# A decay tile in place of a third transpose, and one C Bᵀ burst a block, in a Mamba-2 scan with SwiGLU

## The chip, the cores and the metric

The kernel runs on one core of one Trainium2 chip. The metric is the device time of an execution in microseconds, lower being better. The core has five engines that run their own instruction lists side by side: TensorE (PE, the matrix engine; the profile shows its weight loads apart as PEld), VectorE (DVE), ScalarE (ACT), GpSimd (POOL) and SyncE (SP), which here issues nearly all transfers.[...]

## The reference

There are two parts. The first is a scan with a decaying state (Mamba-2), for 4 batches, 8 heads, 768 steps, 32 values a head (x) and 16 states (B and C). The second is a SwiGLU layer over the 3072 tokens of 256 values that come out of it.

```python
for c in range(nc):                      # chunks of 32 steps
    cum = np.cumsum(la, axis=-1)         # la = log(a), per head
    L = np.exp(cum[..., :, None] - cum[..., None, :]) * causal
    M = np.einsum('bhin,bhjn->bhij', Cc, Bc) * L
    y_intra = np.einsum('bhij,bhjd->bhid', M, xc)
    y_inter = np.einsum('bhin,bhnd->bhid', Cc, state) * np.exp(cum)[..., None]
    y[:, :, sl] = y_intra + y_inter
    Bx = np.einsum('bhjn,bhjd->bhjnd', Bc, xc) * np.exp(cum[..., -1:] - cum)[..., None, None]
    state = np.exp(la.sum(-1))[..., None, None] * state + Bx.sum(2)
# then, on the 3072 x 256 tokens
xn = x / np.sqrt(np.mean(x * x, -1, keepdims=True) + 1e-6) * rms_g
g, val = xn @ w_gate, xn @ w_val         # 256 -> 1536
out = (g / (1 + np.exp(-g)) * val) @ w_out
```

The inputs' weights come as 64-bit numbers in the kernel's view and are turned into fp32 on the chip.

## The kernel before, in words

**Tiling.** Tokens are worked in six blocks of 512 (NBLK). A block is two *pairs*; a pair is two chunks of 128 tokens of one batch, all eight heads side by side (8 heads x 16 states fill the 128 partitions). From pair 2 on, a chunk of 128 is worked as two halves of 64 tokens, so that the masked matrices are 64 x 64. There are 12 pairs, numbered 0 to 11; block b holds pairs 2b and 2b+1.

**A pair's steps**, with the names that the order uses:

- `bc`, `x`: the pair's B, C and x are loaded.
- `scale` (line 484): VectorE makes Bd, B times the decay from each token to the end of its chunk, and Cd, C times the decay from the chunk's start to each token.
- `turn` (line 499): TensorE transposes B, C and (from pair 2 on) Cd of one chunk through the identity into one PSUM bank `tp`, so three transposes a chunk. `T` copies the transposed B and Cd into tile T on ScalarE (line 505), `Tt` the transposed C twice, each time with the heads of one parity set to zero (line 1034, through `turned_of`).
- `g` (line 536): TensorE forms C Bᵀ of all heads of the pair: 16 small products on tiles of 32 x 64 of the array, each issued in two records. The results lie in a pair of banks and two single ones.
- The decay matrices L are made two blocks ahead: `row`/`rowout` store the rows of running sums to DRAM, `spread` loads them back over the partitions, `sub` and `ex` subtract and take the exponential, and GpSimd's select sets what lies ahead of a token to zero.
- `L`, `L1` (lines 556, 562): VectorE multiplies C Bᵀ by L, two heads' pairs at once from the pair of banks and the rest one bank at a time.
- `A` (line 582): TensorE sums Bᵀ x over a chunk's tokens; `S` (lines 596 to 606) carries the state on.
- `y` (line 656): TensorE adds the state's part (from Cdᵀ) and the chunk's own part. The `additions` for pair p+1 are issued at the end of pair p's y, into free columns of the same banks.
- `sq`, `yt`: ScalarE takes squares and copies y out of PSUM; `ms`, `rs`, `xn` norm the tokens of a block.

**The SwiGLU layer.** From block 1 on (and for half of block 0) each group of four products over two row blocks, two columns and two halves of the tokens is formed by seven products of sums (`P.1` to `P.7`, line 844, with `take`, line 850, `C`, line 856, `silu`, line 865, and `hid`, line 869); the output layer does the same (`O.1` to `O.7`, line 934, with sums `s`, `s2`, `s3`, `s4`). The sums of weights are made once (`cw`, line 814, `two`, line 890), those of tokens per block (`tx`). Block 0 also uses plain products (`early`, line 770, `gate`, line 760, `o`, line 876), while `pow`, `man` and `wt` turn the loaded weights into fp32.

**The order.** Nothing is planned at run time: one list, written out by hand, names every step as `block:step`, and each engine gets its instructions in the order of that list. A step `1:turn.0.1` belongs to the next block's pair while block 1's products run, so the scan of block b+1 is laced into the products of block b. SP's transfers stand in the list as well (`fetch` for weights, `bc`, `x`, `spread`, `out`), and one that has to wait for its buffer holds up those behind it. PSUM has two pairs of banks in the first stage (slots 0 and 1, later two for gate and two for val), one further pair (slot 2) and two single banks that all scan steps share.

Of the kernel before, what the change touches and what calls it, by code (L numbers as in the profile page):

```python
# [20 lines left out]
def kernel(  # L21
# [33 lines left out]
    nc = tc.nc  # L55
# [357 lines left out]
    def pair_tile(g):  # L413
        p = g // 2
        if p not in Ls:
            Ls[p] = ssd.tile([P, 2, NH, P if p < 2 else HC], FP32, tag="L", name="L", bufs=2)
        return Ls[p][:, g % 2]
# [60 lines left out]
    def scale(p):  # L478
        s = st[p]
        b, c0 = divmod(2 * p, NC)  # L480
        hs = slice(b * NH, (b + 1) * NH)
        for name, src, d in (("Cd", "C", to_i), ("Bd", "B", from_j)):
            s[name] = ssd.tile([P, 2, NH, N], FP32, tag=name, name=name)
            nc.vector.tensor_tensor(
                out=s[name], in0=s[src],
                in1=d[:, c0:c0 + 2, hs].unsqueeze(3).to_broadcast([P, 2, NH, N]), op=ALU.mult)
# [7 lines left out]
    def turn(p, i, parts=3):  # L494

        s = st[p]
        ps["t", p, i] = tp = bank("tp", (P, parts, P))
        for k, src in enumerate((s["B"], s["C"], s.get("Cd"))[0:parts]):
            nc.tensor.transpose(out=tp[:, k], in_=src[:, i].rearrange("p h n -> p (h n)"),  # L499
                                identity=ident)  # L500

    def turned(p, i, copy):
        tp = ps["t", p, i]
        if tp.shape[1] == 3:
            copy(out=transposed(p)[:, i, 0::3], in_=tp[:, 0::2])
        else:
            copy(out=transposed(p)[:, i, 0], in_=tp[:, 0])

    def turned_of(p, i, t, scaled):

        scaled(transposed(p)[:, i, 1 + t], ps["t", p, i][:, 1], tmask[:, t:t + 1])
# [11 lines left out]
    def product(p, todo):  # L523
        T = st[p]["T"]
        for i in range(2):
            for q, g in todo:
# [8 lines left out]
                for u in halves:  # L535
                    nc.tensor.matmul(  # L536
                        out=g[u, P * i:P * i + P].rearrange("p (t m) -> p t m", t=2),
                        lhsT=T[r, i, 0, u], rhs=T[r, i, 1:3, u], start=(i == 0), stop=True,
# [7 lines left out]
    def products_at_once(p, g):  # L546

        ps["g", p, 0] = g
        ps["g", p, 2], ps["g", p, 3] = g2, g3 = bank("g2", (P, 512)), bank("g3", (P, 512))
        product(p, [(0, g[:, 0]), (1, g[:, 1]), (2, g2), (3, g3)])  # L550

# [92 lines left out]
    def outputs(p, y):  # L644

        if p < 2:
            return first_outputs(p, y)
        s = st[p]
        ps["y pair", p] = y
        y = [y[:, 0], y[:, 1], bank("y2", (P, 512)), bank("y3", (P, 512))]  # L650
        ps["y", p] = y
        first = (2 * p) % NC == 0
        opened = set()

        def product_y(k, u, i, rows, **operands):
            nc.tensor.matmul(out=y[2 * k + u][rows, i * HC:(i + 1) * HC],  # L656
# [4 lines left out]
        for i in range(2):  # L661
            for u in range(2):
                for q in range(NQ):
                    if first and i == 0 and u == 0:
# [13 lines left out]
        if 2 <= p < NPAIR - 1:  # L678
            additions(p + 1, [y[u][:, P:2 * P].rearrange("p (i t d) -> p i t d", i=2, t=2)
                              for u in range(2)])  # L680
        del st[p], Ls[p]

    def parts_of_y(p):
        y = ps["y", p]
        return [(0, slice(0, 2), ps["y pair", p][:, :, 0:P])] + [
            (1, slice(u, u + 1), y[2 + u][:, 0:P].unsqueeze(1)) for u in range(2)]

    def squares(p):
# [3 lines left out]
        tk = slice(half * 256, half * 256 + 256)  # L692
# [5 lines left out]
        sq2 = nrm.tile([P, 2, 2, 2, HC], FP32, tag="sq2", name="sq2", bufs=1)  # L698
        for k, us, y in parts_of_y(p):
            nc.scalar.activation(out=sq2[:, k, :, us].rearrange("p i u m -> p u i m"),  # L700
                                 in_=y.rearrange("p u (i m) -> p u i m", i=2), func=AF.Square)
        s2 = sq2.rearrange("p k i u m -> p k (i u m)")
        nc.gpsimd.tensor_tensor(out=sqs[blk][:, tk], in0=s2[:, 0], in1=s2[:, 1], op=ALU.add)

    def taken_out(p, copy):
# [3 lines left out]
        tk = slice(half * 256, half * 256 + 256)  # L709
# [5 lines left out]
        for k, us, y in parts_of_y(p):  # L715
            copy(out=yts[blk][:, k, tk].rearrange("p (i u m) -> p u i m", i=2, u=2)[:, us],
                 in_=y.rearrange("p u (i m) -> p u i m", i=2))
# [287 lines left out]
    def row_sums(k):  # L1005

        ps["row", k] = r_ps = bank("r_ps", (P, P))
        nc.tensor.matmul(out=r_ps, lhsT=laf[:, 2 * k * BH:(2 * k + 4) * BH], rhs=mid,
                         start=True, stop=True)

    def row_store(k):
        c = 2 * k
        r_sb = nrm.tile([P, P], FP32, tag="r_sb", name="r_sb", bufs=2)
        nc.vector.tensor_copy(out=r_sb, in_=ps.pop(("row", k)))
        nc.sync.dma_start(out=rowd[:, c * BH:(c + 4) * BH].rearrange("u r m -> r u m"),
                          in_=r_sb.rearrange("r (u m) -> r u m", u=2))

# [14 lines left out]
    rowv = rowd.rearrange("u r m -> u (r m)")  # L1032
    def by_scalar(out, in_, scale):
        ac.activation(out=out, in_=in_, func=AF.Copy, scale=scale)

    def by_vector(out, in_, scale):
# [10 lines left out]
        "scale": scale, "turn": lambda p, i: turn(p, i, 3 if p > 1 else 2),  # L1047
        "T": lambda p, i: turned(p, i, ac.copy if p else dv.tensor_copy),
        "Tt": lambda p, i, t: turned_of(p, i, t, by_scalar if p else by_vector),
# [5 lines left out]
        "y": lambda p: outputs(p, take("y", ("y", p))),  # L1055
# [16 lines left out]
        "row": row_sums, "rowout": row_store,  # L1072
# [15 lines left out]
    def of_chunk(n, fn):  # L1088
# [9 lines left out]
        "turn": of_pair(1, turn), "T": of_pair(1, lambda p, i: turned(p, i, ac.copy)),  # L1098
        "Tt": of_pair(1, lambda p, i, t: turned_of(p, i, t, by_scalar)),
        "scale": of_pair(1, scale),  # L1100
        "g": of_pair(1, lambda p: products_at_once(p, pair_of_banks("g", 2))),
        "L": of_pair(1, lambda p: decayed(p, 0)),
        "L1": of_pair(1, decayed_one),
        "A": of_pair(1, additions), "S": of_pair(1, states),
        "y": of_pair(1, lambda p: outputs(p, pair_of_banks("y", 2))),
        "sq": of_pair(1, squares), "yt": of_pair(1, lambda p: taken_out(p, ac.copy)),
# [11 lines left out]
        0:aT 0:la0 0:log4.0.4 0:fetch.7 0:log 0:mask.1.1/2 0:log4.4.2 0:log4.6.2 0:sel 0:upto2  # L1118
        0:after2 0:whole 0:r.0 0:tmask 0:parts.0 0:middles 0:c*2 0:turn.0.1 0:T.0.1 0:cx 0:kinks
        0:eps 0:Tt.0.1.0 0:d 0:dx 0:fetch.8 0:Tt.0.1.1 0:sums.0.1 0:exp.0.1 0:turn.0.0 0:Tt.0.0.0  # L1120
        0:T.0.0 0:Tt.0.0.1 0:scale.1 0:cc 0:sums.0.0 0:exp.0.0 0:mean 0:turn.1.0 0:never16 0:g.0.1/0
        0:L.0.1 0:turn.1.1 0:bc.3 0:T.1.1 0:Tt.1.0.1 0:Tt.1.1.1 0:Tt.1.0.0 0:T.1.0 0:Tt.1.1.0
        0:fetch.9 0:sums.1.1 0:exp.1.1 0:g.0.0/1 0:scale.0 0:last.0 0:Tl.0 0:L.0.0 0:pow.0 0:man.0
        0:A.0 0:S.0 0:bc.4 0:row.1 0:rowout.1 0:man.1 0:wt.0 0:g.1.1/0 0:A.1 0:S.1 0:last.1 0:pow.1
        0:L.1.1 0:Tl.1 0:pow.2 0:mask.1.0/2 0:sums.1.0 0:exp.1.0 0:row.0 0:g.1.0/1 0:mask.3/0
        0:pow.5 0:man.5 0:fetch.10 0:r.1 0:y.0/2 0:sq.0 0:pow.3 0:L.1.0 0:y.1/1 0:sq.1 0:wt.1
        0:scale.2 0:rowout.0 0:man.2 0:pow.6 0:yt.0 0:ydone.0 0:turn.2.0 0:early.0.0/2 0:parts.1
        0:sums.3 0:exp.3 0:ms.0 0:rs.0 0:wt.2 0:pow.4 0:yt.1 0:ydone.1 0:early.0.1 0:mask.2/0
        0:sums.2 0:turn.2.1 0:man.3 0:wt.5 0:wt.3 0:early.1.0/1 0:early.1.1 0:man.4 0:fetch.11
        0:man.6 0:fetch.14 0:scale.3 0:exp.2 0:pow.7 0:xn.0 0:wt.6 0:T.2.0 0:T.2.1 0:Tt.2.1.0  # L1130
        0:Tt.2.1.1 0:Tt.2.0.0 0:Tt.2.0.1 0:table.0 0:x.3 0:wt.4 0:gate.2/0 0:man.8 0:man.7
        0:fetch.13 0:norm.0 0:norm.1 0:wt.7 0:gg.2/2 0:L1.2.3 0:L1.2.2 0:silu.0 0:hid.0 0:L.2.0
        0:tx.0 0:gate.3/1 0:pow.9 0:silu.2 0:hid.2 0:man.9 0:fetch.15 0:A.2 0:S.2 0:pow.8 0:wt.8
        0:silu.3 0:hid.3 0:wt.9 0:pow.10 0:man.11 0:cw.3 0:gate.4/2 0:silu.4 0:hid.4 0:man.10
        0:pow.11 0:wt.11 0:turn.3.1 0:turn.3.0 0:T.3.0 0:Tt.3.0.1 0:T.3.1 0:Tt.3.0.0 0:Tt.3.1.1
        0:Tt.3.1.0 0:wt.10 0:switch.0 0:P.1.3 0:take.1.3 0:x.4 0:gate.5/1 0:silu.5 0:hid.5
        0:fetch.12 0:pow.12 0:y.2/2 0:spread.10 0:spread.11 0:S.3 0:sq.2 0:yt.2 0:ydone.2 0:P.6.3
        0:take.6.3 0:man.13 0:man.12 0:switch.1 0:P.2.3 0:P.1.4 0:pow.13 0:gg.3/2 0:L.3.0 0:L1.3.2
        0:L1.3.3 0:P.2.4 0:silu.1 0:scale.4 0:C.11.3 0:silug.11.3 0:take.1.4 0:fetch.19 0:P.7.3
        0:wt.12 0:take.7.3 0:y.3/2 1:S.0 0:sq.3 0:yt.3 0:ydone.3 0:spread.8 0:P.5.3 0:C.22.3  # L1140
        0:silug.22.3 0:pow.14 0:P.4.3 0:silug.21.3 0:tok 0:tokout 0:P.3.3 0:cw.4 0:P.6.4 0:ms.1
        0:fetch.18 0:wt.13 0:take.6.4 0:C.12.3 0:P.2.5 0:silug.12.3 0:pow.15 0:C.11.4 0:silug.11.4
        0:P.5.4 0:P.7.4 0:take.7.4 0:fetch.16 0:man.14 0:wt.14 0:o.0/2 0:pow.16 0:hid.1 0:o.1
        0:P.4.4 0:silug.21.4 0:cw.5 0:hidg.22.3 0:hidg.11.3 0:hidg.12.3 0:C.22.4 0:hidg.21.3 0:P.1.5
# [173 lines left out]
```

## Time and profile before

| | |
|---|---|
| median of 3 runs | 409.12 us (409.10 to 409.29) |
| the profiled execution | 409.49 us, of which the span 407.4 |
| TensorE busy | 399.9 us (98%) |
| VectorE busy | 303.7 us (75%) |
| ScalarE busy | 231.9 us (57%) |
| GpSimd busy | 37.5 us (9%) |
| moved by DMA | 23.91 MB |

Times in the views are microseconds from the span's start. A row of a list of instructions gives start, duration (first start to last end), engine, line, operation, tile written from tiles read, and the count of records. A row of the groups gives count, then busy time, mean duration in ns, then the engine's idle time just before them and what ended it. Ends on TensorE are modelled and matmuls overlap, so that its rate is read from starts. A 32-bit matmul stands as two records.

### The profile page before, as it was taken

What the parts mean: (1) busy time and instruction counts of PE and PEld (TensorE: products, weight loads), DVE (VectorE), ACT (ScalarE), POOL (GpSimd) and SP (SyncE); (2) the same over time, 40 slices, a digit from 0 to 9 for tenths busy, and PEclk for the clock granted to TensorE, in tenths of its full rate; (3) what the DMA queues carried; (4) which work ended last, traced back from release to release, by engine and by line L of the source; (5) the groups of instructions that cost most, each with busy time, mean ns of one, the idle gap of its engine ahead of it and who ended that gap; (6) DMA issues with size and microseconds to landing.
All of it is one profiled execution on the core that took longest, in us unless ns stands there. A gap on an engine that the chain in (4) does not pass through costs nothing.

```text
span 407.4 us, 9550 instructions
## 1 busy us (share of the span) xinstructions
PE 399.9 (98%) x3867; PEld 340.4 (84%) x3867; DVE 303.7 (75%) x698; ACT 231.9 (57%) x506; POOL 37.5 (9%) x61
## 2 busy tenths in 40 slices
PE   8999999999899999999999999999999999999997
PEld 4566577888688899888899988899988899988997
DVE  5999999898976787856799278779455777265863
ACT  3899989795556445664584355534566442453500
POOL 4010000003200001300023000001300000000000
PEclk9999999999999999999999999999999999999999
DMA  9998937400401171302080501020300000100001
GB/s 112 231 213 173 266 118 209 53 0 5 75 0 28 29 126 39 44 1 55 20 131 8 79 2 53 2 80 2 77 2 0 2 4 0 53 1 2 0 2 52
DMA packets 87371, 23.91 MB, mean 59 GB/s; under 512 B 76800, under 2 KB 81152, under 8 KB 87328
## 3 DMA queue, kind: packets, MB, share of 16 engines
q1 hardware_dynamic: 83168, 23.05, 26.9%
q10 hardware_dynamic: 4160, 0.26, 0.8%
q8 instruction: 30, 0.49, 0.5%
q14 instruction: 13, 0.11, 0.1%
HBM read 20.02 MB, written 3.28 MB: 57 GB/s over the span
## 4 chain that ended last, share of the span: by engine, by line
PE 90%; DVE 4%; ACT 3%; DMA 1%; issue 1%; SPq 0%; ACTq 0%
PE gate L844 27%; PE o L934 22%; PE val L844 20%; PE o L876 4%; PE gate L760 3%; PE y L656 3%; PE tp L499 2%; PE gate L770 2%; PE g L536 1%; PE ms L725 1%; DVE sw L814 1%; DVE s L907 1%; DMA L<-rowd 1%; PE e L422 1%; ACT e L183 1%
## 5 line engine op out<-in xcount | busy, mean ns | idle before, releaser
L856 DVE TENSOR_TENSOR c<-val,p 128x512 f32<-128x512 f32 x99 | 67.6, 688 | 46.3 <-PE val L844 27.5
L850 ACT COPY p<-gate 128x512 f32<-128x512 f32 x99 | 57.4, 586 | 52.4 <-PE gate L844 49.2
L844 PE MATMUL gate<-tx,sw 128*128 128x256 f32 x264 | 65.5, 381 | 0.0
L865 ACT ACTIVATE c<-c 128x256 f32<-128x256 f32 x99 | 39.9, 417 | 41.8 <-DVE c L856 41.6
L844 PEld LDWEIGHTS gate<-tx,sw 128*128 128x128 f32 x264 | 49.1, 190 | 7.0 <-ACT p L850 0.3
L869 DVE TENSOR_TENSOR h<-c 128x256 f32<-128x256 f32 x99 | 41.4, 433 | 17.4 <-ACT c L865 17.3
L844 PE MATMUL val<-tx,sw 128*128 128x256 f32 x132 | 33.9, 381 | 1.2 <-DVE c L856 1.2
L844 PE MATMUL val<-xn,wgv 128*128 128x256 f32 x132 | 34.1, 380 | 0.0
L844 PE MATMUL gate<-xn,wgv 128*128 128x256 f32 x132 | 34.0, 382 | 0.0
L844 PE MATMUL val<-xn,sw 128*128 128x256 f32 x132 | 33.9, 381 | 0.0
L844 PE MATMUL gate<-tx,wgv 128*128 128x256 f32 x132 | 33.8, 383 | 0.0
L471 POOL TENSOR_SCALAR_AFFINE_SELECT L<-L 64x512 f32<-64x512 f32 x32 | 23.5, 734 | 83.3 <-ACT L L469 72.9
L934 PEld LDWEIGHTS o<-two,s 128*128 128x128 f32 x240 | 28.3, 192 | 1.9 <-issue 1.4
L934 PE MATMUL o<-wo,h 128*128 128x128 f32 x240 | 29.5, 275 | 0.0
L934 PE MATMUL o<-two,s 128*128 128x128 f32 x240 | 29.3, 276 | 0.1
L934 PEld LDWEIGHTS o<-wo,h 128*128 128x128 f32 x240 | 28.4, 192 | 0.7 <-DVE h L869 0.2
L934 PE MATMUL o<-two,h 128*128 128x128 f32 x240 | 28.9, 275 | 0.0
L844 PEld LDWEIGHTS val<-tx,sw 128*128 128x128 f32 x132 | 24.7, 190 | 5.0 <-DVE c L856 1.6
L844 PEld LDWEIGHTS gate<-tx,wgv 128*128 128x128 f32 x132 | 24.4, 190 | 4.2 <-ACT p L850 0.6
L934 PEld LDWEIGHTS o<-two,h 128*128 128x128 f32 x240 | 27.8, 192 | 0.0
L844 PEld LDWEIGHTS val<-xn,wgv 128*128 128x128 f32 x132 | 24.5, 190 | 3.9 <-DVE c L856 0.6
L844 PEld LDWEIGHTS val<-xn,sw 128*128 128x128 f32 x132 | 24.6, 190 | 3.5 <-DVE h L869 0.2
(179 smaller groups left out, 645.9 us busy)
## 6 DMA issues: line engine op xcount, KB each, us to landing
L<-rowd SPq DMA_DIRECT2D x32, 128.0 KB, 3.2
xr<-in_x_dram SPq DMA_DIRECT2D x24, 128.0 KB, 4.2
wr<-in_moe_w_out_dram SPq DMA_DIRECT2D x6, 512.0 KB, 5.0
wr<-in_moe_w_gate_dram SPq DMA_DIRECT2D x5, 512.0 KB, 5.8
wr<-in_moe_w_val_dram SPq DMA_DIRECT2D x5, 512.0 KB, 5.9
out_dram<-ob SPq DMA_DIRECT2D x9, 256.0 KB, 2.2
br<-in_B_dram SPq DMA_DIRECT2D x22, 64.0 KB, 3.8
cr<-in_C_dram SPq DMA_DIRECT2D x22, 64.0 KB, 3.1
```

The costliest lines, as they stand in the source:

```text
L471: nc.gpsimd.affine_select(out=L[r], in_=L[r], pattern=[[0, NH], [1, HC]], compare_op=ALU.is_ge, fill=0.0, base=0, channel_multiplier=-1)
L499: nc.tensor.transpose(out=tp[:, k], in_=src[:, i].rearrange("p h n -> p (h n)"), identity=ident)
L656: nc.tensor.matmul(out=y[2 * k + u][rows, i * HC:(i + 1) * HC], start=(k, u, rows.start) not in opened, stop=True, skip_group_check=True, ...
L760: nc.tensor.matmul(out=gv[:, k], lhsT=w[:, t, fs], rhs=xns[0][:, t], start=(t == 0), stop=(t == 1))
L770: nc.tensor.matmul(out=gv[:, k, tk], lhsT=w[:, t, fs], rhs=yts[0][:, t, tk], start=(s == 0 and t == 0), stop=(t == 1), skip_group_check=True)
L844: nc.tensor.matmul(out=dst[:, half[w]], lhsT=lhsT, rhs=rhs, start=(k in (1, 2, 5) and w == 0), stop=True, skip_group_check=True)
L850: nc.scalar.copy(out=t, in_=Xs[j])
L856: nc.vector.tensor_tensor(out=t, in0=Zs[j], in1=a, op=ALU.add)
L865: nc.scalar.activation(out=u, in_=src[:, half[0]], func=AF.Silu)
L869: nc.vector.tensor_tensor(out=hidden_tile(blk, j)[:, c // 10 - 1, c % 10 - 1], in0=u, in1=src[:, half[1]], op=ALU.mult)
L876: nc.tensor.matmul(out=o, lhsT=hs_[blk, f // 2][:, f % 2, k // 2, (k % 2) * P:(k % 2 + 1) * P], rhs=wo[:, f], start=opens, stop=(f == NF - ...
L934: nc.tensor.matmul(out=o[t] if apart else o[:, t * P:(t + 1) * P], lhsT=lhsT[:, t], rhs=rhs, start=(k in (1, 2, 4, 5) and j == 0 and (apar ...
```

## The change

For pairs 2 to 11 Cd is no longer formed and no longer transposed. In its place a tile of decays, already laid out as Cdᵀ needs them (heads and states on the partitions, tokens along the row), is loaded (`dT`) and multiplied with the transposed C on VectorE (`Td`). The rows of decays come from a second product in `row` and an exponential on ScalarE, stored to a DRAM array `rowe` (step `rowe`).

A pair's four transposes (B and C of both chunks) go into one bank, and are copied out with one `T` and two `Tt`. From block 2 on, C Bᵀ of both pairs of a block is one burst (`g`), weighted by L per block; y is issued in a burst per pair, but both pairs write into the same banks, and `sq` and `yt` take the whole block. The additions of pair p+2 are issued in y of pair p. In block 1 the first of these (pair 3) go with pair 2 and those of pairs 4 and 5 with pair 3.

The list of steps is unchanged up to its 39th entry and in a new order from there; it has 1543 steps in place of 1585.

```diff
-        for name, src, d in (("Cd", "C", to_i), ("Bd", "B", from_j)):
+        for name, src, d in (("Cd", "C", to_i), ("Bd", "B", from_j))[0 if p < 2 else 1:]:
...
+    def turn(p, i=None):
         s = st[p]
+        if i is None:
+            ps["t", p] = tp = bank("tp", (P, 2, 2, P))
+            for k, src in enumerate((s["B"], s["C"])):
+                for i in range(2):
+                    nc.tensor.transpose(out=tp[:, k, i],
+                                        in_=src[:, i].rearrange("p h n -> p (h n)"),
+                                        identity=ident)
+            return
...
+    def spread_decays(p):
+        b, c0 = divmod(2 * p, NC)
+        st.setdefault(p, {})["dT"] = d = ssd.tile([P, 2, P], FP32, tag="Cd", name="dT")
+        nc.sync.dma_start(
+            out=d.rearrange("p i m -> p (i m)"),
+            in_=rowe[b * NH:(b + 1) * NH, c0 * P:(c0 + 2) * P].unsqueeze(1).to_broadcast(
+                [NH, N, 2 * P]))
+
+    def turned_decayed(p):
+        nc.vector.tensor_tensor(out=transposed(p)[:, :, 3], in0=ps["t", p][:, 1], in1=st[p]["dT"],
+                                op=ALU.mult)
...
+    def products_of_block(blk, g):
+
+        ps["g", blk] = gs = [g[:, 0], g[:, 1], bank("g2", (P, 512)), bank("g3", (P, 512))]
+        ps["g pair", blk] = g
+        for k in range(2):
+            product(2 * blk + k, [(q, gs[q][:, 256 * k:256 * k + 256]) for q in range(NQ)], k == 0)
...
-        if 2 <= p < NPAIR - 1:
-            additions(p + 1, [y[u][:, P:2 * P].rearrange("p (i t d) -> p i t d", i=2, t=2)
-                              for u in range(2)])
+        for k, p2 in enumerate(after):
+            cols = slice((width + n + k) * P, (width + n + k + 1) * P)
+            additions(p2, [y[u][:, cols].rearrange("p (i t d) -> p i t d", i=2, t=2)
+                           for u in range(2)])
...
-        ps["row", k] = r_ps = bank("r_ps", (P, P))
-        nc.tensor.matmul(out=r_ps, lhsT=laf[:, 2 * k * BH:(2 * k + 4) * BH], rhs=mid,
-                         start=True, stop=True)
+        ps["row", k] = r_ps = bank("r_ps", (P, 2, P))
+        for j, rhs in enumerate((mid, upto)):
+            nc.tensor.matmul(out=r_ps[:, j], lhsT=laf[:, 2 * k * BH:(2 * k + 4) * BH], rhs=rhs,
+                             start=(j == 0), stop=True, skip_group_check=True)
...
+    def row_decays(k):
+        c = 2 * k
+        r_sb = nrm.tile([P, P], FP32, tag="r_sb", name="e_sb", bufs=3)
+        nc.scalar.activation(out=r_sb, in_=ps["row", k][:, 1], func=AF.Exp)
+        nc.sync.dma_start(out=rowe.rearrange("h (c m) -> c h m", m=P)[c:c + 4], in_=r_sb)
```

## The prediction

> **What bounds the kernel now.** I read the page's busy shares and its chain of waits first, then ten-microsecond windows, then the list of TensorE instructions in order of time, then the groups with shapes kept apart.
>
> ```profile
> span 407.4 us, 9550 instructions
> ...
> PE 399.9 (98%) x3867; PEld 340.4 (84%) x3867; DVE 303.7 (75%) x698; ACT 231.9 (57%) x506; POOL 37.5 (9%) x61
> ...
> PE 90%; DVE 4%; ACT 3%; DMA 1%; issue 1%; SPq 0%; ACTq 0%
> ```
>
> TensorE is busy 98% of the span and makes 90% of the chain that ended last. The windows say where the other engines still matter (columns: PE, PEld, DVE, ACT and POOL busy, then clock, DMA share, GB/s):
>
> ```profile
> 20.00:30.00 10.00, 9.02 (x151) 6.01 (x148) 9.79 (x22) 9.28 (x16) 1.46 (x2) 1.00 0.93 214
> ...
> 90.00:100.00 10.00, 10.00 (x48) 8.81 (x47) 8.55 (x18) 5.92 (x9) 1.70 (x3) 1.00 0.00 0
> 100.00:110.00 10.00, 8.77 (x70) 6.90 (x69) 9.37 (x19) 6.77 (x16) 4.36 (x6) 1.00 0.44 81
> ...
> 300.00:310.00 10.00, 10.00 (x49) 8.81 (x48) 5.04 (x11) 6.93 (x19) 0.00 (x0) 1.00 0.01 2
> ```
>
> There are two regimes. Up to about 110 us VectorE is at 9 tenths or more and can starve TensorE. After that TensorE is full and VectorE has a quarter to a half of its time free; every TensorE microsecond taken out there shortens the run, as long as no new wait appears. The clock is 1.00 throughout, so it is no term of the sum.
>
> A busy TensorE still hides the price of changing its tile shape, because the ends of its records overlap. That price is read from starts:
>
> ```profile
> 133.08 1.89 PE L844 MATMUL gate<-tx,sw 128*128 128x256 f32 x8
> 134.81 1.03 PE L844 MATMUL val<-tx,sw 128*128 128x256 f32 x4
> 135.77 0.69 PE L536 MATMUL g<-T 32*64 32x128 f32 x32
> 136.39 1.13 PE L844 MATMUL gate<-tx,wgv 128*128 128x256 f32 x4
> 137.36 1.03 PE L844 MATMUL val<-xn,sw 128*128 128x256 f32 x4
> ...
> 148.59 0.27 PE L499 MATMUL tp<-ident,br 128*128 128x128 f32 x1
> 148.70 0.27 PE L499 MATMUL tp<-ident,cr 128*128 128x128 f32 x1
> 148.81 0.27 PE L499 MATMUL tp<-ident,Cd 128*128 128x128 f32 x1
> 148.92 1.02 PE L725 MATMUL ms<-sq,mean 128*128 128x512 f32 x2
> ```
>
> Eight records from 133.08 to 134.81 give 0.216 us each. The four at 134.81 should be over at 135.67, and the g burst starts at 135.77: 0.10 to get in. It holds the engine 0.62 (to 136.39), and the next four records take 0.97 in place of 0.86: 0.11 to get out. One g burst costs 0.83 us. A transpose costs the engine 0.11 (148.59, .70, .81, .92), not its 0.27 duration.
>
> **The change part by part.**
>
> *Third transpose.* Pairs 2 to 11 each lose two transposes of Cd: 20 records x 0.11 = 2.2 us off TensorE. The Trainium skill ("TensorE: Matmul & The Clock Gate", Part 4: PE-mode transpose) prices a 128x128 transpose at about 275 ns inside a kernel. The trace has that as its duration (273 ns), but the next one starts 109 ns later. By the page the saving is 20 x 0.275 = 5.5 us and the forecast below would be 402.3; I take the pitch, since starts and not durations fill the engine.
>
> *One g burst a block.* In blocks 2 to 5 two bursts become one with 64 records. 32 records on eight positions are four passes of 128 columns; a pass of that width costs 0.11 (the transposes), so the second pair adds 0.44. The new burst is 0.83 + 0.44 = 1.27 against 1.66: 0.39 saved, times 4 = 1.5 us. Bounds: 0 if the engine drains between the pairs after all, 1.9 if the second pair's last pass also hides in the way out. I take 1.5. Outputs remain a burst per pair; the additions go with pair p+2 in place of p+1, as many as before: nothing.
>
> *Row sums.* Two matmuls 128x128 more, two records each: 4 x 0.11 = +0.45 us (they lie before 30 us, where some of it falls into idle time; 0 to 0.6).
>
> *Other engines.*
>
> ```profile
> L1034 ACT ACTIVATE T<-tp,tmask 128x128 f32<-128x128 f32 x44 | 14.0, 379 | 2.0 <-PE tp L499 2.0
> ...
> L505 ACT COPY T<-tp 128x256 f32<-128x256 f32 x20 | 7.4, 372 | 1.3 <-PE tp L499 1.3
> ...
> L562 DVE TENSOR_TENSOR L<-g,L 128x256 f32<-128x256 f32 x20 | 8.0, 418 | 3.3 <-PE g L536 3.2
> ...
> L484 DVE TENSOR_TENSOR Cd<-cr,d_sb 128x256 f32<-128x256 f32 x12 | 5.0, 415 | 0.0
> ```
>
> On VectorE the ten scalings by 0.415 go and ten products of the transposed C with the decay tile come, shape like L562's 0.418: even. The weighting by L, two times (0.68 + 2 x 0.418) = 3.03 a block, becomes 1.22 + 2 x 0.68 = 2.58. On ScalarE two copies of 0.372 and four scaled copies of 0.379, 2.26 a pair, become one copy and two wider ones of about 0.49: 0.9 saved a pair. Yt and squares go from 12 records a block to 6. Two Exp of 128x128 (about 0.3) are added. All of this lies beside TensorE after 110 us and is worth nothing there; before 110 us it helps ScalarE, which is not the tightest, and leaves VectorE as it is.
>
> *The decay tile's way.* It takes a store and then a load through DRAM on SP's queue:
>
> ```profile
> L<-rowd SPq DMA_DIRECT2D x32, 128.0 KB, 3.2
> ...
> rowd<-r_sb SPq DMA_DIRECT2D x2, 64.0 KB, 2.3
> ```
>
> Here a rule speaks against the change: the Trainium skill ("DMA: Bandwidth & Descriptors", Anatomy of one DMA) gives a DMA of the GpSimd path a fixed cost of about 2.0 us whatever its size, most of it until the written data is acknowledged; taken over to SP's queue, as an estimate, the detour takes at least 4 us, 4.5 with the bytes. The rows, for just such a pair, make it 2.3 + 3.2 = 5.5; I use that. For pair 2 the order puts early.1.0, early.1.1 and gate.2 (2 x 1.73 + 3.43 = 6.9 us of TensorE) and a turn between the load's issue and the product with it: covered, with about a microsecond and a half to spare. Behind dT.2 on SP stand the loads of pairs 3 and 4, rowout.0 and fetch.10, none needed for ten microseconds. If the tile is late, Td waits at the head of VectorE, and behind it stand the weighting by L and the weights of the next gate; with VectorE full, each late microsecond would be one on TensorE. The tight place later is pair 7: its tile takes pair 6's buffer, so the load can go only after Td of pair 6; 3.2 us stand against four groups of products, 3.4 us. I count nothing, 0 to 1 us.
>
> *New order.* It first differs at the 40th step. Three effects:
>
> At the border of blocks 0 and 1 TensorE stands still:
>
> ```profile
> 103.16 1.89 PE L844 MATMUL gate<-tx,sw 128*128 128x256 f32 x8
> 106.28 1.13 PE L844 MATMUL val<-tx,sw 128*128 128x256 f32 x4 [1.23 <-DVE c L856]
> ```
>
> Eight records should end at 104.89: 1.39 us lost, behind combinations of weights on VectorE (0.87 each while POOL's selects run, 0.41 after). The new order moves the subtractions ahead, and pair 4's weighting by L later; but it puts scaling of pair 5 (0.46) and its states (two of 0.29, four of 0.28: 1.7) into block 0. I take half, -0.7 (bounds -1.4 to +1.5).
>
> At the start the first product with normed-later tokens (early.0.0, 26.18 us) waits for yt.0 on VectorE. By a count of VectorE's rows ahead of it in either order it comes 0.4 us sooner. The second half (early.0.1) comes later, since man.6 (1.1) and wt.2 (0.42) now stand ahead of yt.1 while less TensorE work lies between: about 0.8 us lost. Net +0.4 (bounds -2, from the some 8 us of idle before 26 us, to +2).
>
> ScalarE's loads of function tables, 1.28 us each, are 19 in the trace; by the order of the functions the new list has two fewer, three of the rest for a table already there. Hidden.
>
> **Sum.** -2.2 - 1.5 + 0.45 - 0.7 + 0.4 = -3.55 us. The profiled execution took 409.49 (span 407.4 and 2.1 around it), so its like would take 405.9; against the median of 409.12 that is **405.6**. Times within 0.2% (0.8 us: 408.3 to 409.9) count as no change; that is about what this kernel's runs can tell apart.
>
> **The rivals.**
>
> *A wait in place of the removed work* (14%). The rotation of two single banks and one pair of banks is now held from a block's first output burst to its last copy, and the late decay products keep the transposes' bank. For it: the list has Td of pair 6 only after the turn of pair 7. Against it: after 110 us VectorE is at 5 to 9 tenths, and the bursts have five or more groups of products (4.3 us) ahead of their use. Half a microsecond in each of four blocks, or a g burst that saves nothing: 407.5.
>
> *More than the work* (14%). The start's idle time shrinks by 1.2 and the border's stall goes entirely (0.7 more): 403.7.
>
> *Slower: VectorE starves TensorE before 110 us* (12%). One mechanism: in the windows from 10 to 70 us VectorE is 91 to 99% busy, so order alone decides whether weights are ready; the added 2.2 us of block-1 work in block 0 and yt.1 put back push gate.2 and what follows. It decides from 3.3 us plus 0.8 of more idle; at 4.5 us net of the border's relief it gives 410.4. Against it: counted through to gate.2 the new list is behind by only 0.8 us.
>
> *It does nothing measurable* (5%): the same, with a loss of 3 to 4: 408.9. That the work isn't removed at all is excluded, since the transposes are no longer issued.
>
> **How the numbers follow.** The forecast case has 55%, with its own range 404.4 to 406.8 (g 0 to 1.9 and the border's bounds, not all at one end). Faster is 55 + 14 + 14 = 83%, same 5%, slower 12%. The range reaches from 403.2 (some of the larger gain left out below) to 408.4 (the slower and the unchanged case left out above).
>
> **What would show it.** TensorE's records fall by 20 and rise by 4: 3851. tp<-ident,Cd is left with pairs 0 and 1 only; four g bursts of 64 records each take 1.06 from first start to the next product. TensorE stays at 98%; a share below 97% speaks for a wait, and the window shows where: before 30 us or at 100 us the order, beside g, y or tp the banks. ScalarE should fall by some 15 us, VectorE by 2. The prediction is wrong if TensorE's idle time before 110 us grows by more than 2 us, or if the second pair in a g burst costs 0.8 rather than 0.44.

## The result, and the profile after

The changed kernel takes **407.67 us** (median of 11 runs, 405.95 to 408.68) beside 409.22 us for the kernel before (11 runs, 408.71 to 410.72): a ratio of 0.995, 95% interval 0.9931 to 0.9969, or 1.3 to 2.8 us less. The forecast was 405.6: the direction is right, and 1.5 to 2 us of the gain are missing. The time lies inside the whole range of the forecast (403.2 to 408.4) and outside that of its main case (404.4 to 406.8). Its profiled execution took 407.43 us (409.49 before).

The page of the changed kernel, the lines that answer to those shown of before:

```profile
span 405.7 us, 9479 instructions
...
PE 398.3 (98%) x3851; PEld 340.1 (84%) x3851; DVE 300.1 (74%) x686; ACT 220.9 (54%) x451; POOL 36.6 (9%) x57
...
PE 84%; SPq 4%; DVE 4%; DMA 4%; ACT 2%; issue 1%; ACTq 0%; DVEq 0%
```

TensorE has the 3851 records that were forecast and is still busy 98% of the span. The new thing is in the last line. The chain of waits before had 1% DMA and nothing to speak of from SP's queue; now these two make 8% of it. Most of that is loads before 26.5 us, to which the chain leads back through the decay tile's two transfers:

```profile
32.41 2.94 DMA rowe<-e_sb
...
36.02 4.45 DMA dT<-rowe
```

The decay tile's way has come onto the path that sets the end.

The stretch of the border in the trace (columns as before: PE, PEld, DVE, ACT, POOL busy, clock, DMA share, GB/s):

```profile
100.00:110.00 10.00, 10.00 (x47) 8.62 (x46) 8.44 (x18) 6.81 (x15) 4.25 (x6) 1.00 0.01 2
```

From 100 to 110 us TensorE is now busy for all ten microseconds, where it had 8.77: the stall at the border of blocks 0 and 1 is gone. Two smaller stretches show where time was lost instead. First before, then the changed kernel:

```profile
32.00:44.00 12.00, 12.00 (x103) 6.89 (x99) 11.90 (x24) 11.78 (x20) 0.00 (x0) 1.00 0.89 203
...
56.00:72.00 16.00, 15.95 (x211) 12.43 (x210) 15.59 (x37) 14.43 (x35) 1.46 (x2) 1.00 0.74 208
```

```profile
32.00:44.00 12.00, 11.48 (x103) 6.86 (x103) 10.57 (x20) 11.23 (x18) 0.00 (x0) 1.00 0.89 177
...
56.00:72.00 16.00, 15.21 (x230) 11.33 (x229) 15.57 (x38) 12.54 (x33) 1.74 (x2) 1.00 0.83 186
```

TensorE, full in both before, now lacks 0.52 and 0.79 us there, and VectorE lacks 1.4 us from 32 to 44. The first of the losses, in VectorE's list and then in TensorE's, which shows the cheap parts as well:

```profile
40.57 0.42 DVE L536 TENSOR_TENSOR T<-tp,dT 128x256 f32<-128x256 f32 x1 [0.70 <-ACT e L182]
```

```profile
40.16 0.46 PE L562 MATMUL g<-T 32*64 32x128 f32 x12
41.14 0.65 PE L562 MATMUL g<-T 32*64 32x128 f32 x20 [0.52 <-DVE T L536]
...
130.63 1.21 PE L562 MATMUL g<-T 32*64 32x128 f32 x64
131.77 1.13 PE L891 MATMUL val<-tx,sw 128*128 128x256 f32 x4
...
155.15 0.38 PE L505 MATMUL tp<-ident,br 128*128 128x128 f32 x2
155.37 0.38 PE L505 MATMUL tp<-ident,cr 128*128 128x128 f32 x2
155.59 1.02 PE L772 MATMUL ms<-sq,mean 128*128 128x512 f32 x2
```

Line 536 in VectorE's list is `Td`, the product of the transposed C with the decay tile. For pair 2 it starts at 40.57 after 0.70 us of waiting. The wait is put down to ScalarE's `e`, which is needless to `Td`; what landed just before it is the decay tile, at 40.47 (36.02 + 4.45). In TensorE's list the g burst of pair 2 breaks off after 12 of its 32 records, four for each of its first three banks, and goes on at 41.14, with `Td` as the releaser. It doesn't read what `Td` writes: its fourth bank, g3, is the single bank that held the transposes, and `Td` has yet to read them there. The burst holds TensorE 1.56 us in place of 0.62.

Further down, the merged g burst takes 1.14 us from its first start to the next product (forecast 1.06), and four transposes take 0.44 (155.15 to 155.59), 0.11 each, as the pitch (the time from one start to the next) said.

The transfers behind that:

```profile
24.66 2.24 SPq L121 DMA_DIRECT2D cr<-in_C_dram  x1
26.95 4.10 SPq L121 DMA_DIRECT2D br<-in_B_dram  x1
31.11 0.57 SPq L121 DMA_DIRECT2D cr<-in_C_dram  x1
31.78 0.53 SPq L1063 DMA_DIRECT2D rowd<-r_sb  x1
32.41 0.68 SPq L1070 DMA_DIRECT2D rowe<-e_sb  x1
...
35.40 0.53 SPq L1070 DMA_DIRECT2D rowe<-e_sb  x1
36.02 0.62 SPq L530 DMA_DIRECT2D dT<-rowe  x1
```

These are SP's own instructions. The four loads of `bc.4` stand ahead of the first stores of rows. Issuing them takes SP from 23.72 to 31.68, two of them 2.24 and 4.10 us each, where the last takes 0.57. So the first decay rows, which ScalarE had made by 22.05 us, leave at 32.41. The second half leaves at 35.40, when the first has landed (35.35), and the tile's load stands behind it, at 36.02; it lands 4.45 us later.

### The profile page after: what moved, and what is told of

The parts are those of the page before. It is cut to its first block, busy times and chain, and to the rows that moved or that the text cites. A ratio compares the mean times of both kernels' runs of the same rounds, so it can differ in the third digit from the quotient of the medians.

```text
span 405.7 us, 9479 instructions
## 1 busy us (share of the span) xinstructions
PE 398.3 (98%) x3851; PEld 340.1 (84%) x3851; DVE 300.1 (74%) x686; ACT 220.9 (54%) x451; POOL 36.6 (9%) x57
## 4 chain that ended last, share of the span: by engine, by line
PE 84%; SPq 4%; DVE 4%; DMA 4%; ACT 2%; issue 1%; ACTq 0%; DVEq 0%
PE gate L891 28%; PE o L981 23%; PE val L891 21%; PE o L923 5%; PE y L699 3%; SPq L121 2%; SPq L128 1%; PE g L562 1%; DMA wr<-in_moe_w_gate_dram 1%; DMA dT<-rowe 1%; PE ms L772 1%; PE tp L505 1%; DMA br<-in_B_dram 1%; SPq L160 1%; DVE h L840 1%; DMA rowe<-e_sb 1%
## 5 line engine op out<-in xcount | busy, mean ns | idle before, releaser
L916 DVE TENSOR_TENSOR h<-c 128x256 f32<-128x256 f32 x99 | 40.1, 418 | 16.1 <-ACT c L912 16.0
L997 ACT COPY v<-o 128x256 f32<-128x256 f32 x15 | 5.7, 377 | 41.9 <-PE o L981 41.9
```

The source lines that it names most:

```text
L916: nc.vector.tensor_tensor(out=hidden_tile(blk, j)[:, c // 10 - 1, c % 10 - 1], in0=u, in1=src[:, half[1]], op=ALU.mult)
L997: nc.scalar.copy(out=ts[k], in_=halves_of(Os["X"]))
```

## The experiments

The theory that this trace suggests: TensorE's savings are all there, and about 2.7 us go in block 0, to the decay tile being late behind `bc.4` (a) and to three later waits for banks: the turn of pair 3 at 56.8, y of pair 3 at 61, and `tok` at 66.9 (b). The rival: VectorE and ScalarE set the pace of block 0, and a wait removed there comes back elsewhere. A second rival doubts the savings themselves.

A table of traces first, since the runs are read by it. It gives, from the starts of TensorE's instructions, the start of pair 2's transposes, the time from there to pair 3's, from pair 3's to pair 4's, and from pair 4's to TensorE's end (us).

| kernel | pair 2's turn at | to pair 3's | to pair 4's | to the end |
|---|---|---|---|---|
| changed | 32.56 | 24.20 | 14.91 | 331.04 |
| changed (a0_after) | 32.43 | 23.57 | 15.19 | 331.04 |
| changed (a1_after) | 32.56 | 25.08 | 15.08 | 331.08 |
| e3_bc4_later | 32.51 | 23.15 | 14.92 | 331.02 |
| e3b_bc4_later | 32.51 | 23.15 | 15.10 | 330.94 |
| e4_banks | 32.59 | 24.66 | 19.63 | 331.23 |
| e5_all | 32.28 | 22.81 | 19.15 | 331.15 |
| e7_moves | 32.19 | 22.81 | 15.50 | 331.27 |
| e9_three_moves | 34.28 | 23.14 | 14.91 | 331.07 |
| e1_g_split | 34.02 | 23.14 | 14.92 | 332.39 |

The last column differs by 0.33 us at most where the later blocks are the same, so that all that moves is in the three before it. Three executions came to pair 2 some 1.5 us later than the others (e9_three_moves and e1_g_split here, and e2_two_transposes); they began late, as the last section shows, whatever the kernel.

**The changed kernel again.**

> The changed kernel again, as the yardstick for the runs beside it. 0.995 of the time before, some 2.0 us less; four stalls of TensorE before 70 us, at the g burst of pair 2 (0.9 us), the turn of pair 3 (0.6), y of pair 3 (0.6) and the sum tok (0.7).

> The changed kernel again, beside the two below on one chip: 0.9945 (0.9935 to 0.9955) by all theories.

Measured: 407.71 us (ratio 0.9941, interval 0.9919 to 0.9962) and 407.99 us (0.9952, 0.9934 to 0.9970), beside the kernel before on the same chip. The effect stands. Its traces add that the loss differs from execution to execution: 23.57, 24.20 and 25.08 us for the same 24 us of work. In the last of them the row behind it is on VectorE:

```profile
35.85 0.29 DVE L1062 COPY r_sb<-r_ps 128x128 f32<-128x128 f32 x1 [2.11 <-DMA rowd<-r_sb]
```

and on TensorE:

```profile
38.15 3.67 PE L807 MATMUL gate<-xn,wgv 128*128 128x512 f32 x8 [1.48 <-DVE wgv L201]
41.75 0.91 PE L562 MATMUL g<-T 32*64 32x128 f32 x32
```

The rows of sums and the rows of decays share a tile with three buffers (`r_sb`). There were two such rows before; now there are four, and the fourth copy waits at the head of VectorE until the first store has landed. That store stands behind `bc.4` too. Behind the copy are the weights of the next gate, so that TensorE stands 1.48 us. In the first trace of the changed kernel the same copy waits only 0.53 us, and there the g burst pays.

**The loads of pair 4 moved back.** `bc.4` behind `bc.3`, nothing else:

```diff
-        ... 0:g.0.0/1 0:L.0.0 0:bc.4 0:man.1 0:pow.0
+        ... 0:g.0.0/1 0:L.0.0 0:man.1 0:pow.0
...
-        ... 0:man.7 0:bc.3 0:turn.2 0:T.2 ...
+        ... 0:man.7 0:bc.3 0:bc.4 0:turn.2 0:T.2 ...
```

> Loads of pair 4's B and C moved from ahead of the store of decays to behind the first decay tile's load. Theory (the decay tile is late because SP's queue is backed up by these loads; Td waits on it, and the g burst of pair 2 needs the bank that Td reads): the store rowe is issued by about 28 us in place of 32.4, the tile lands by 36, Td does not wait, and the g burst of pair 2 holds TensorE 0.62 us in place of 1.56: 0.9 us less than the changed kernel. Rival (VectorE is the limit before 80 us, so a stall taken away comes back further on): the g burst is short, and the end moves by less than 0.3 us.

> bc.4 behind bc.3 again, to tell it from the changed kernel with more rounds. If the late decay tile cost time in the changed kernel: 0.3 to 0.8 us under the changed kernel of this call, so 0.9930. If the wait at 40 us is made up before TensorE is dense (at 67 us): the same ratio as the changed kernel, within 0.0005.

Measured: 406.52 us (0.9933, 0.9908 to 0.9959), and in the second run 406.40 us (0.9916, 0.9899 to 0.9934) beside 407.99 for the changed kernel. SP's instructions, the copy and `Td` in the second run, and then TensorE's burst:

```profile
23.14 0.70 SPq L1063 DMA_DIRECT2D rowd<-r_sb  x1
23.93 0.68 SPq L1070 DMA_DIRECT2D rowe<-e_sb  x1
...
30.29 0.53 SPq L1070 DMA_DIRECT2D rowe<-e_sb  x1
30.91 0.63 SPq L530 DMA_DIRECT2D dT<-rowe  x1
```

```profile
33.62 0.28 DVE L1062 COPY r_sb<-r_ps 128x128 f32<-128x128 f32 x1
...
39.14 0.40 DVE L536 TENSOR_TENSOR T<-tp,dT 128x256 f32<-128x256 f32 x1
```

```profile
39.99 0.69 PE L562 MATMUL g<-T 32*64 32x128 f32 x32
```

The first decay rows leave 8.5 us sooner, the tile's load 5.1 us sooner, neither the copy nor `Td` waits, and the g burst is whole. From pair 2's turn to pair 3's it is 23.15 us in both runs: 0.4, 1.1 and 1.9 us less than in the three traces of the changed kernel, 1.1 on the mean. The difference of the medians in the second run, 1.6 us, is larger; all six of its executions lie between 406.2 and 406.4 us, the lower of the two groups that the last section describes, so I go by the 1.1 of the traces. Part (a) of the theory holds: 0.9 us was expected in the first run and 0.3 to 0.8 in the second. The chain of waits has no transfer left in it:

```profile
PE 94%; DVE 4%; issue 1%; ACT 1%; DVEq 0%; ACTq 0%
```

By its medians this is the fastest kernel of the study.

One row of the table shows the same mechanism from the other side. e1_g_split has `bc.4` in its old place, and still takes 23.14 us from pair 2's turn to pair 3's. TensorE came to the turn 1.5 us later there and SP did not: the tile's load is issued at 35.08, neither the copy nor `Td` waits, and the g burst is whole at 41.49. So the late tile costs time in executions that begin early, as all three traces of the changed kernel do, and nothing in this one, which began late.

**The bank waits, first try.** Three steps moved back, so that what holds the banks is copied out first:

```diff
 (moved, each to behind the step named)
+        0:pow.12  behind 0:ydone.2
+        0:man.13  behind 0:L1.3.2
+        0:tok 0:tokout  behind 0:take.1.4
```

> Three steps of block 0 moved out of the way: the powers of weight piece 12 behind the copies of y of pair 2, the mantissas of piece 13 behind the weighting by L of pair 3, and the sum tok two steps later. Theory (TensorE waits for the two single PSUM banks, which ScalarE and VectorE let go late): the turn of pair 3, y of pair 3 and tok wait no more; 0.6 + 0.6 + 0.7 = 1.9 us less than the changed kernel. Rival (VectorE is the limit before 80 us): less than 0.6 us, with new waits between 65 and 110 us.

> All four moves together. Theory: 0.9 + 1.9 = 2.8 us less than the changed kernel, a ratio of about 0.988 to the kernel before, near 404.8 us where the kernel before has 409.2. Rival: a ratio of 0.993 or more.

The second kernel has these and the move of `bc.4`. Measured: 410.97 us (1.0023, 1.0008 to 1.0037) and 410.13 us (1.0011, 0.9997 to 1.0025). Neither gain came. The rival had asked for 0.993 or more in e5_all, which holds to the letter only, since both kernels have a new stall that the moves made. In e4_banks, on ScalarE:

```profile
57.20 0.81 ACT L182 ACTIVATE e<-wr,kinks 128x512 int16<-128x512 int16 x1
...
59.42 0.56 ACT L897 COPY p<-gate 128x512 f32<-128x512 f32 x1
```

and on TensorE:

```profile
60.04 1.39 PE L891 MATMUL gate<-tx,sw 128*128 128x256 f32 x4 [2.14 <-ACT p L897]
61.23 1.91 PE L891 MATMUL val<-xn,wgv 128*128 128x256 f32 x4
```

The three steps of `pow.12` (lines 182 to 185, 2.2 us) now stand just ahead of `take.1.3`, the copy that frees a bank of gate for P.6.3, and TensorE waits 2.14 us for it. I had weighed what the step was moved past and not what stood behind its new place. What follows costs as much again: the four records from 61.23 are about 0.43 us apart and not 0.216 (the last section), and two waits of 0.8 us each come later. From pair 3's turn to pair 4's it is 19.63 and 19.15 us in place of about 15. So these two kernels do not tell what the three waits cost.

**The bank waits, second try.** Five moves, with the places chosen by what stands behind them:

```diff
 (moved, each to behind the step named)
+        0:bc.4  behind 0:bc.3
+        0:pow.12  behind 0:take.6.3
+        0:man.13  behind 0:scale.5
+        1:S.1  behind 0:C.22.3
+        0:tok 0:tokout  behind 0:P.3.3
```

> The changed kernel with five moves in block 0: loads of pair 4 behind the first decay tile's load; powers of weight piece 12 behind the copy take of the sixth product (not ahead of the first one's, which cost 2.3 us in the run before); mantissas of piece 13 behind the two scalings; states of pair 5 behind the total C.22; the sum tok behind the third product. Theory (four late releases in block 0 took back what the removed work gave): the stalls of TensorE at g of pair 2, the turn of pair 3, y of pair 3 and tok go, 2.0 to 2.8 us less than the changed kernel, a ratio to the kernel before of 0.988 to 0.989. Rival (VectorE is full there and the stall comes back elsewhere): 0.993 or more.

Measured: 407.12 us (0.9935, 0.9912 to 0.9958), where the rival had 0.993 or more. The waits at the g burst, at the turn of pair 3 and at `tok` are gone, and y of pair 3 holds TensorE 2.06 us in place of 2.41. From pair 2's turn to pair 3's it is 22.81 us, 0.34 less than with `bc.4` moved alone; from there to pair 4's it is 15.50, some 0.5 more. P.4.3 now waits for `take.7.3`, which comes after `pow.12`:

```profile
64.43 1.13 PE L891 MATMUL gate<-tx,wgv 128*128 128x256 f32 x4 [0.47 <-ACT p L897]
```

One more run leaves `pow.12` where the changed kernel has it and keeps the other four moves.

> Of the five moves of the earlier run all but pow.12's, which stays where the changed kernel has it: bc.4 behind bc.3, man.13 behind scale.5, 1:S.1 behind C.22.3, tok and tokout behind P.3.3. If each wait of block 0 is a matter of place: those of g of pair 2, y.3 and tok go, no new one comes since take.7.3 is not behind pow.12, and the time is 1.4 to 1.9 us under the changed kernel of this call, ratio 0.9905. If VectorE and ScalarE are the bound up to 67 us: the waits come back elsewhere, and it is at most 0.6 us under the changed kernel, ratio 0.9930 or more.

Measured: 407.19 us (0.9936, 0.9913 to 0.9959). TensorE has no wait of over 0.35 us left between its groups of instructions from pair 3's turn to pair 4's, and still that stretch takes 14.91 us, the same as in the changed kernel. The fair partner is e1_g_split, which began late too and has none of the moves: 14.92 us, and 23.14 for both in the stretch before. Within the later stretch the rival holds: the moves traded a few waits that one can see for many small ones. In the stretch ahead of it a wait was removed and stayed away. The early and the late part of block 0 behave differently.

**The g burst split again.** Each of the four merged bursts is issued as two with one group of products between; all else as in the changed kernel:

```diff
-        for k in range(2):
-            product(2 * blk + k, [(q, gs[q][:, 256 * k:256 * k + 256]) for q in range(NQ)], k == 0)
+        second_of_block(blk, 0)
+
+    def second_of_block(blk, k=1):
+        gs = ps["g", blk]
+        product(2 * blk + k, [(q, gs[q][:, 256 * k:256 * k + 256]) for q in range(NQ)], k == 0)
...
-        1:hid.11.4 1:P.6.5 1:take.6.5 1:P.2.5 1:C.11.5 1:g 1:L1.2 1:L1.3 1:L 1:P.5.4 1:P.7.5
+        1:hid.11.4 1:P.6.5 1:take.6.5 1:g 1:P.2.5 1:C.11.5 1:gs 1:L1.2 1:L1.3 1:L 1:P.5.4 1:P.7.5
...
```

> Each C B^T burst of a block is issued as two bursts of a pair with a group of products between; all else as in the changed kernel. By the trace one burst of 64 records holds TensorE 1.137 us and costs 0.20 at its edges, two of 32 cost 2 x (0.622 + 0.20): each block should lose 0.30 us, the run 1.2 us against the changed kernel (ratio to the kernel before about 0.998). If the merging gained nothing, no difference.

Measured: 409.37 us (0.9994, 0.9977 to 1.0011). The last column of the table has it without what happens in block 0: 332.39 us in place of 331.05, so the merging is worth 1.34 us, 0.34 a burst (1.2 were expected).

```profile
130.17 0.69 PE L562 MATMUL g<-T 32*64 32x128 f32 x32
130.79 1.13 PE L894 MATMUL val<-xn,wgv 128*128 128x256 f32 x4
131.86 0.69 PE L562 MATMUL g<-T 32*64 32x128 f32 x32
```

Two bursts of 0.62, each with 0.21 to get in and out, make 1.66; the merged one makes 1.14 + 0.21 = 1.35.

**The third transpose alone.** The kernel before with two transposes for each chunk. It leaves the decay out of the state's part of y, which is then formed from the plain transposed C; the scaling of C on VectorE and the order stay:

```diff
-        "scale": scale, "turn": lambda p, i: turn(p, i, 3 if p > 1 else 2),
+        "scale": scale, "turn": lambda p, i: turn(p, i, 2),
```

> The kernel before with the third transpose left out for pairs 2 to 11; the state's part of y is then formed from the transposed C without its decay, so that this part of the output is left out. All else, order and copies, is unchanged. Theory (TensorE is full, so work removed shortens the run by its pitch): 20 x 0.109 = 2.2 us less than the kernel before, ratio 0.9946. Rival (the time removed turns into waits for VectorE in block 0 and elsewhere): 1.0 us or less, ratio 0.9975 or more.

Measured: 408.13 us (0.9957, 0.9943 to 0.9972), 1.8 us less by the ratio. In the trace, from pair 2's second turn to `tok` the time falls from 31.53 to 31.27 us, and from there to the end from 340.66 to 338.96: 1.96 in all, with 19 of the 20 transposes in these two stretches (2.07 by the pitch of 0.109). The pitch is confirmed; the duration of 273 ns, 5.5 us for the 20, is ruled out as the price.

**The border alone.** The kernel before with `two.0` of block 1 (four subtractions of output weights) moved behind the total `C.11.0` that TensorE waits for:

```diff
-        1:Tt.0.1.1 0:table.1 1:cw.2 1:two.0 1:P.2.0 1:C.11.0 1:silu.11.0 ...
+        1:Tt.0.1.1 0:table.1 1:cw.2 1:P.2.0 1:C.11.0 1:two.0 1:silu.11.0 ...
```

> The kernel before with the first combination of output weights (two.0, four subtractions) moved behind the total that TensorE waits for at 104.7 us. Theory (that stall is VectorE's queue): the stall of 1.39 us at 104.7 us goes, 1.4 us less than before, ratio 0.9966. Rival: it comes back within the next products, no difference.

Measured: 407.98 us (0.9962, 0.9949 to 0.9975), 1.6 us less by the ratio.

```profile
103.17 1.89 PE L844 MATMUL gate<-tx,sw 128*128 128x256 f32 x8
104.90 1.03 PE L844 MATMUL val<-tx,sw 128*128 128x256 f32 x4
```

The products follow on each other. From the turn at 102 us to the next one at 121 it is 17.60 us, where the kernel before has 19.11: 1.51. The stall was the order of VectorE's list, and it can be taken away whole.

## Why the prediction was right in its direction and short in its size

*Third transposes, -2.2.* Right: 20 records fewer, 0.109 apart; alone 1.8 to 2.0 us.

*Merged g bursts, -1.5.* Nearly right: -1.34 (the split run), 0.34 a burst. The second pair adds 0.515 and not 0.44: 1.137 - 0.622. The sentence that 32 records are four passes of 0.11 was a little too low.

*Row sums, +0.45, and the start, +0.4.* Measured together by the start of gate.2, behind both: 36.32 us before, 36.56 after. With the two transposes that pair 2 lost ahead of it (-0.2) the row sums' 0.45 is all of it, and the start's order counts for nothing. early.0.0 starts 0.63 us sooner (26.18 to 25.55) and early.0.1 at the same time (29.63 to 29.61), not 0.8 later. The "some 8 us of idle before 26 us" behind the bound there is misread: TensorE is busy for 22.79 of these 26 us, which leaves 3.2.

*Border, "I take half, -0.7".* Too cautious: the stall of 1.39 is gone whole, and alone is worth 1.5.

*The decay tile's way, "I count nothing, 0 to 1 us".* **This is the step that failed.** I reckoned with one store and one load, 2.3 + 3.2 us, from the place that they have in the list, and checked what stands behind the load on SP. I didn't work out when SP can issue them. The four loads of `bc.4` ahead of the stores hold SP for 8 us, and the trace of before shows the same for its first store of rows:

```profile
22.98 2.17 SPq L121 DMA_DIRECT2D cr<-in_C_dram  x1
25.20 3.19 SPq L121 DMA_DIRECT2D br<-in_B_dram  x1
...
30.83 2.53 SPq L121 DMA_DIRECT2D br<-in_B_dram  x1
33.40 1.56 SPq L121 DMA_DIRECT2D cr<-in_C_dram  x1
35.06 0.53 SPq L1015 DMA_DIRECT2D rowd<-r_sb  x1
```

There it was hidden, because L is needed later (its first loads from these rows are issued at 54.55). In the changed kernel only 4.1 of the 6.9 us of TensorE work that were to cover the way were left when the load was issued (36.02, the burst at 40.16), and the way itself is longer: 8.06 us from the first store's issue to the tile's landing in place of 5.5, made of 2.94 for the store, 0.67 for the second store ahead of the load, and 4.45 for the load. The consequence I gave ("Td waits at the head of VectorE, each late microsecond one on TensorE") was right. It comes on two more ways: a bank that `Td` must read before g3 may be written, and a fourth row on three buffers. Against the run with `bc.4` moved it costs 0.4 to 1.9 us in the three traces, 1.1 on the mean, which is above the bound of 1. The other tight place that I named, pair 7, cost nothing that shows: TensorE is busy for all 290 us from 110 to 400.

*What is left.* The parts as measured make -1.96 - 1.34 - 1.51 + 0.45 = -4.4, which is 0.8 more than the -3.55 forecast, since the border gave twice what I took. TensorE's end came from 404.67 to 402.71 us: -2.0. Block 0 therefore gives back 2.4. That the time still fell inside the whole range owes something to luck: the border's extra gain covered part of a loss that I had put at nothing. In this trace 0.94 go at the g burst, 0.42 at the turn of pair 3, some 0.35 in y of pair 3 and 0.72 at `tok`, together 2.4; before had about 0.2 at `tok` and 0.2 after y of pair 3 itself, so the match is rougher than it looks. The first is shown to be the queue's. For the other three, two other orders took most of the waits away and not the time: from pair 2's turn to pair 4's it is 38.31 us with the five moves and 38.05 with four, beside 38.07 and 38.25 with `bc.4` alone. VectorE is at 15.57 of 16 us in the stretch from 56 us on, but it was at 15.59 before, when TensorE was full there; that it is VectorE's work as such wasn't tried. The cause of this part, some 1.3 us, stays open.

*The rivals.* "A wait in place of the removed work" has the time about right (407.5) and one of the waits, the late decay product that keeps the transposes' bank. But it placed them in four blocks, after 110 us, and there TensorE is dense. The slower rival (VectorE starves TensorE before 110 us, deciding from 3.3 us plus 0.8) has the place and part of the mechanism, at 2.4 us of its 4.1. "More than the work" had the border right.

*What would show it.* 3851 records, tp<-ident,Cd left with the first pairs and four bursts of 64 came as told. VectorE fell by 3.6 us (told: 2). ScalarE fell by 11.0 and not 15: the copies of the transposes did as told,

```profile
L1089 ACT ACTIVATE T<-tp,tmask 128x256 f32<-128x256 f32 x20 | 8.6, 484 | 0.0
```

0.484 against the 0.49 taken. But I added durations, and busy time counts the overlap of one instruction with the next once. The durations of ScalarE's groups (count times mean) add up to 261.3 us before and 244.3 after, 17.0 less (three table loads of 1.28 among them, 19 to 16, one more than told); 55 instructions fewer take 6.0 us of overlap away with them. None of it is on the path. TensorE's idle time before 110 us went from 4.7 to 4.4 us, so the mark set for a wrong prediction (2 us more) wasn't reached, although block 0 lost 2.4: the border's 1.2 us of idle went at the same time, and part of the loss lies within bursts that count as busy.

## What to carry to other kernels

A transfer through DRAM is to be costed from the moment its queue can issue it: list what stands ahead of the store and of the load, with the issue times that the trace of before shows for those very loads, before adding the time to landing. Count the buffers of every tile that gets more users, and ask for each new reader of a shared bank who writes that bank next. A step put ahead of a copy that frees a bank can cost its whole length on the matrix engine (2.2 us of ScalarE's work, 2.14 us of waiting here); in the stretch of block 0 where VectorE is full, moving waits about bought nothing.

## What the runs showed of the hardware

*A stall of two microseconds can cost more than itself.* After the wait of 2.14 us in e4_banks, in stretches of two microseconds (TensorE's granted clock is the third column from the end):

```profile
60.00:62.00 2.00, 1.96 (x6) 1.68 (x7) 0.42 (x1) 1.53 (x5) 0.00 (x0) 0.69 0.59 111
62.00:64.00 2.00, 2.00 (x35) 1.09 (x33) 0.00 (x0) 1.94 (x4) 0.00 (x0) 0.50 1.05 299
64.00:66.00 2.00, 2.00 (x38) 1.32 (x28) 1.70 (x5) 0.21 (x1) 0.00 (x0) 0.95 0.98 93
```

The clock is at half in the middle stretch. What is missing from 1.00 in the three makes 1.7 us of full-speed work, that is 3.4 us at half. In the trace of e5_all, after 2.13 us, it is the same (0.76, 0.50, 0.89). But it isn't so in every execution: the core's mean clock is 0.995 or 0.996 in 11 of the 22 executions of each of these kernels (1.7 us of 411 are 0.004) and 1.00 in the other 11, and the medians of the two halves are 1.2 us apart in e4_banks and 0.8 in e5_all. What decides isn't shown. The Trainium skill ("TensorE: Matmul & The Clock Gate", Part 1, HAM oscillation) warns of gaps of more than some 3.4 us between matmuls. Here 2.1 us were enough in half of the executions, while 1.48 us in the trace of a1_after left the clock at 1.00; the measurement decides, and a stall of two microseconds may have to be counted at nearly twice its length.

*Executions begin in two ways, 1.5 us apart.* Of the kernel e6_border, nine executions lie between 407.6 and 408.3 us and five from 408.5 to 409.4; e3_bc4_later has four from 406.2 to 406.6 and two at 408.0. In the changed kernel the groups run together, which fits the late tile, whose cost falls on executions that begin early. The profiled ones differ between 6 and 10 us: in e9_three_moves, e1_g_split and e2_two_transposes the first matmuls take nearly twice as long, and pair 2's turn comes some 1.5 us later (the table's first column; 33.91 in e2_two_transposes beside 32.48 before). In e2_two_transposes:

```profile
6.10 1.19 PE L355 MATMUL r_ps<-mids,la 128*128 128x256 f32 x2
...
7.51 1.49 PE L396 MATMUL full_ps<-la,chunk_ones 128*128 128x192 f32 x4
```

In the first trace of the changed kernel the same two take 0.67 and 0.87 us. The granted clock is shown as 1.00 in both, so that only the rate of the matmuls betrays it. The same page (Part 1, What's actually happening) says that the clock is released by a free-running window of about 3.4 us of activity, so that the count of slow first matmuls differs from run to run; as an estimate from that figure, one window more at half rate loses 1.7 us, and the traces show 1.4 to 1.7. That fits, but no record here shows a lower clock in those microseconds, so the cause is argued and not shown. Differences of under a microsecond are therefore read here from stretches of the trace, between executions that began alike, and the medians only support them.
